# Packed attention before two gated layers: V in long runs, exponentials turned on VectorE, six weight tiles kept on chip

## The chip, the cores and the metric

The kernel runs on one core of one Trainium2 chip. The metric is device time in microseconds (us) of one execution. Five engines run their own in-order queues: TensorE (PE; its weight loads are shown apart as PEld), VectorE (DVE), ScalarE (ACT), GpSimd (POOL) and SyncE (SP), which here issues every copy. Copies run on 16 copy engines beside them.

## What is computed

In float32 inputs, q, k and v are [8, 8, 576, 64] (batch, heads, rows, columns), p is [8, 8, 32, 64]; the weights come in as 8-byte floats and are narrowed on the chip.

```python
def sm_attn(qq, kk, vv):
    s = scale * np.matmul(qq, kk.transpose(0, 1, 3, 2))
    s = s - np.max(s, axis=-1, keepdims=True)
    a = np.exp(s)
    a = a / (np.sum(a, axis=-1, keepdims=True) + 1e-09)
    return np.matmul(a, vv)
p_packed = sm_attn(p, k, v)            # 32 packed rows for each head
out = sm_attn(q, p_packed, p_packed)
x = out.transpose(0, 2, 1, 3).reshape(4608, 512)
xn = x / sqrt(mean(x * x) + 1e-6) * rms_g
x = (silu(xn @ w_gate) * (xn @ w_val)) @ w_out
h = x @ w2_in
result = (h * cos(h)) @ w2_out
```

## The kernel before

The work comes in three parts. The first part turns k, v and p into the packed rows: 16 groups, each of four heads of one batch. The second is the main loop, 192 steps (8 batches x 12 slices of 128 hidden columns x 2 halves of 288 tokens), whose matmuls are the gv products (L173 to L175 by the helper `mm3`) and the acc products. The third is the second layer (hx, ops).

The first part's order is written out by hand: `KEY_ORD` is a list of words, and each word calls one small step. For group i: `K` and `V` load k and v, `p` and `o` turn p and copy it to `pT`, `k` and `q` transpose k on TensorE in three pieces (L411) and evict each by ScalarE (L418), `s` makes the scores (L430, L434), `m` their maximum on VectorE (L441), `e` the exponential on ScalarE (L448), `t` and `T` transpose the exponentials on TensorE (L457) in two blocks of three and evict them by ScalarE (L463), `r` makes the reciprocal of the sum, `P` the product with v (L477), `C` scales it (L485), `f`, `F` and `G` turn it (L493) and put it away. Other words serve the main loop: `L` loads a piece of weights, `a` and `b` narrow it (one ScalarE pass, three VectorE passes, L160 to L168), `c` and `d` split a piece of w_out in two parts, `A` is one step of the second attention of batch 0, `U` makes one unit of batch 0's projected weights (mps, L606), `Z` issues the stores that wait, among them the narrowed weight tiles `wy` (L619), which later batches fetch again. The words are executed in the order of the list, so that every engine's queue and SP's queue hold their instructions in that order.

V is loaded into one of three tiles of 128 partitions, at partitions 16 to 111: 96 partitions with runs of six rows, 1536 bytes for each head (L376). The rest of a V tile and the margins of the one tile of exponentials are zeroed once, and each transpose of `t` takes 128 columns of which 96 are keys. The products of `P` run over 128 partitions, and four heads go to four column groups of the array. The first `S_PAD` = 6 groups make their scores with padded weights (128 columns, L430), the later ones with 32 columns for each head (L434). Float32 products are two instructions each.

Every `wy` tile lives in a ring of four buffers and is stored as soon as it is narrowed. In the main loop, `U_AT` says in which step a unit is made, `B0_W` which piece of weights is loaded and narrowed in which of the first steps, `ATT_FROM0` and `ATT_TO0` between which steps the next batch's attention is spread.

Of the kernel before, what the change touches and what calls it, by code (L numbers as in the profile page):

```python
# [20 lines left out]
def kernel(  # L21
# [39 lines left out]
    V_P = 16  # L61
# [3 lines left out]
    S_PAD = 6  # L65
    KEY_ORD = (
# [17 lines left out]
    )  # L84
    KEY_END = "b13 b14"
    U_AT = {3: (0, 3), 8: (0, 4), 14: (0, 5), 16: (1, 0), 18: (1, 1), 20: (1, 2), 22: (1, 3), 26: (1, 4), 30: (1, 5)}
    U_J = (12, 15, 18, 21, 26, 30)
    B0_W = (15, 16, 17, 18, 19, -4, 20, 21, -5, 22, 23, -6, 0, -7, 0, -8, 0, -9, 0, -10, 0, -11)
# [12 lines left out]
    ATT_FROM, ATT_TO, ATT_FROM0, ATT_TO0, N_ATT = 0, 48, 10, 45, 32  # L101
# [17 lines left out]
    c_dram = [dram.tile([128, 2, D], F32, name=f"c_{b}") for b in range(B)]  # L119
# [112 lines left out]
    def att_load_c(b):  # L232
        nc.sync.dma_start(out=cl, in_=c_dram[b])

    def attend(b):
        NB = HALF // NP
        s = a1.tile([128, 2, 2, NB, NP], F32, tag="s", name="s")
        for g in range(2):
            qTs = []
            for j in (2 * g, 2 * g + 1):  # L240
                qv = qn.pop(4 * b + j)
                qT = a2.tile([128, 2, HALF], F32, tag="qT", name="qT")
                for i in range(2):
                    tp = psb[0].tile([128, HALF], F32, tag="mm", name="qtp")
                    for c in range(CH):
                        nc.tensor.transpose(
                            tp[:, c * CP:(c + 1) * CP], qv[:, i, 2 * c:2 * c + 2, :].rearrange("p c d -> p (c d)"),
                            ident[:CP, :CP],
                        )
                    nc.scalar.activation(out=qT[:, i], in_=tp, func=AF.Copy)  # L250
                    qTs.append(qT[:, i])
                    if i == 0:
                        yield
                if b:
                    load_q()
                yield
            sp = [psb[0].tile([128, HALF], F32, tag="mm", name="sp") for _ in range(2)]
            for h in range(4):
                for r, rows in enumerate((top, bot)):
                    nc.tensor.matmul(  # L260
                        sp[r][h * NP:(h + 1) * NP], bq[rows, 4 * g + h], qTs[h ^ g][rows], start=True, stop=True
                    )
            st = a2.tile([128, 2, NB, NP], F32, tag="st", name="st", bufs=1)
            for r in range(2):
                nc.vector.transpose(st[:, r].rearrange("p c n -> p (c n)"), sp[r])
            yield
            sv = st.rearrange("p r c n -> p (r c) n")
            mx = a2.tile([128, 2 * NB], F32, tag="amx", name="amx")
            nc.vector.tensor_reduce(out=mx, in_=sv, op=ALU.max, axis=AX.X)
            nc.vector.tensor_tensor(  # L270
                out=s[:, g].rearrange("p r c n -> p (r c) n"), in0=sv,
                in1=mx.unsqueeze(2).to_broadcast([128, 2 * NB, NP]), op=ALU.subtract,
            )
            yield
# [77 lines left out]
    v_t = [u2.tile([128, 4, NC_, D], F32, tag=f"vn{x}", name="vn", bufs=1) for x in range(3)]  # L352
    for x in range(2):
        nc.vector.memset(v_t[x], 0.0)
    e_pad = u2.tile([128, 2 * V_P + S], F32, tag="e", name="e", bufs=1)
    for x in (slice(0, V_P), slice(V_P + S, 2 * V_P + S)):
        nc.vector.memset(e_pad[:, x], 0.0)
# [13 lines left out]
    def load_v(i):  # L371
# [3 lines left out]
        vn = nat_v[i] = v_t[i % len(v_t)]  # L375
        nc.sync.dma_start(out=vn[V_P:V_P + CP], in_=v[b, 4 * g:4 * g + 4].rearrange("h (p c) d -> p h c d", c=NC_))  # L376

# [3 lines left out]
    for x, y in ((slice(0, 4), slice(0, 4)), (slice(4, 8, 2), slice(5, 8, 2)), (slice(5, 8, 2), slice(4, 8, 2))):  # L381
        nc.gpsimd.tensor_copy(gS[:, x], gT[:, y])
# [14 lines left out]
    def u_pt(i):  # L397
        pt = st[i]["pt"]
        if i % 2:
            pv, tv = (x.rearrange("p (j r) n -> p j r n", r=2) for x in (pT[:, :, :NP], pt.rearrange("p (h n) -> p h n", h=4)))  # L400
            for r in range(2):
                nc.vector.tensor_copy(pv[:, :, r], tv[:, :, 1 - r])
        else:
            nc.vector.tensor_copy(pT[:, :, :NP], pt.rearrange("p (h n) -> p h n", h=4))
# [10 lines left out]
    def u_kt(i, m):  # L415
        z = st[i]
        kv = z["kT"].rearrange("q h (t p m) -> q h t m p", t=CH, m=CH)
        nc.scalar.activation(  # L418
            out=kv[:, :, :, m, :], in_=z["kp", m].rearrange("q (t h p) -> q h t p", t=CH, h=4), func=AF.Copy
        )  # L420

    def u_s1(i):
# [4 lines left out]
        for h in range(4):  # L427
            for r, rows in enumerate((top, bot)):
                if i < S_PAD:
                    nc.tensor.matmul(  # L430
                        s1[:, r, :HALF], pz[rows, h * 128:(h + 1) * 128], kT[rows, h ^ i % 2], start=h == 0, stop=h == 3
                    )
                else:
                    nc.tensor.matmul(  # L434
                        s1[h * NP:(h + 1) * NP, r, :HALF], pT[rows, h, :NP], kT[rows, h ^ i % 2], start=True, stop=True
# [8 lines left out]
    def u_e(i):  # L444
        z = st[i]
        s1, mx = z["s1"], z["mx"]
        e = e_pad[:, V_P:V_P + S].rearrange("p (a s) -> p a s", a=2)
# [4 lines left out]
    def u_et(i, hf):  # L452
        z = st[i]
        et = z["et", hf] = ps_2.tile([128, CH, 128], F32, tag="kp", name="et")
        for c in range(CH):
            cc = hf * CH + c
            nc.tensor.transpose(et[:, c, :], e_pad[:, cc * CP:cc * CP + 128], ident)  # L457

    def u_ec(i, hf):
        z = st[i]  # L460
        if hf == 0:
            z["eT"] = u2.tile([128, NC_, 128], F32, tag="eT", name="eT", bufs=1)
        nc.scalar.activation(out=z["eT"][:, hf * CH:(hf + 1) * CH], in_=z["et", hf], func=AF.Copy)  # L463
# [6 lines left out]
    def u_pp(i):  # L470
# [3 lines left out]
        for c in range(NC_):  # L474
            for h in range(4):
                r = slice(h * NP, (h + 1) * NP)
                nc.tensor.matmul(  # L477
                    pp[r], eT[:, c, r], vn[:, h ^ i % 2, c % CH * 2 + c // CH, :], start=c == 0, stop=c == NC_ - 1
                )

    def u_c(i):
# [6 lines left out]
        stores.append((c_dram[b][:, g, :], cd[:, 0, :]))  # L488
# [47 lines left out]
    def wy_prep(n, part, x=None):  # L536
        t, j = divmod(n, 2)
        if j == 0 and part == 0:
            w_y[t] = wm_p.tile([128, 2, 512], F32, tag="wy", name="wy", bufs=4)
# [3 lines left out]
        if j and part and x in (None, 3):  # L543
            stores.append((wy_dram[t], w_y[t]))
# [52 lines left out]
    def unit(b, u):  # L597
# [4 lines left out]
        for j in range(2):  # L602
            for r, rows in enumerate((top, bot)):
                for kt in range(2):
                    h = 2 * j + (1 - r if kt else r)
                    nc.tensor.matmul(  # L606
                        ps[kt][h * NP:(h + 1) * NP], ppT[b // 4][rows, 4 * kt + h, n:n + NP],
# [13 lines left out]
    stores = []  # L621
# [9 lines left out]
    def att0_load():  # L631
# [5 lines left out]
        "p": u_prep, "o": u_pt, "k": u_kp, "q": u_kt, "s": u_s1, "m": u_mx, "e": u_e, "t": u_et, "T": u_ec, "r": u_r,  # L637
# [11 lines left out]
    nc.gpsimd.memset(v_t[2], 0.0)  # L649
# [298 lines left out]
    for i in range(len(seq) + LAG):  # L948
# [27 lines left out]
        store(0)  # L976
        if i in units:
# [277 lines left out]
```

## Time and profile before

| | |
|---|---|
| median of three runs | 1615.98 us (1612.12 to 1622.82) |
| profiled execution | 1617.2 us |
| its span, first to last instruction | 1615.4 us |
| mean granted TensorE clock | 0.99 of full speed |
| first gv product of the main loop | 130.34 us after the span's start |

A profile page gives the busy time of each engine, then the costliest groups of instructions by line. A line of the trace names the line of the kernel, the engine, the operation, the tile written and the tiles read, partitions x elements, and a count. "Idle before" is the engine's idle time just before an instruction, with what ended it. A copy's share of 1.00 means that all 16 copy engines are busy all the time; shares can come out a little over 1 because packets overlap.

### The profile page before, as it was taken

Reading aid. Unit: us, or ns where it says so; the run is one execution under the profiler, and the core shown is the slowest. Engines: PE = TensorE matmul, PEld = TensorE weight load, DVE = VectorE, ACT = ScalarE, POOL = GpSimd, SP = SyncE. Lnnn points to the kernel's source line nnn. Section 1 sums busy time; section 2 is a strip of 40 time slices with the busy share of each in tenths; the row PEclk is TensorE's granted clock in tenths of the full one; section 3 lists DMA queues with packets and bytes.
Section 4 is the critical chain, followed back from the end, with each engine's and each line's share of the span. In section 5 each row is a group of like instructions: output and inputs, shape, how many; then the busy total and the mean of one; then the engine's idle time right before and its main releaser. Section 6 shows DMA issues by size and latency. Waiting matters only on the chain.

```text
span 1615.4 us, 28947 instructions
## 1 busy us (share of the span) xinstructions
PE 1570.9 (97%) x11216; PEld 1337.4 (83%) x11216; DVE 977.0 (60%) x1915; ACT 897.8 (56%) x1796; POOL 34.0 (2%) x49
## 2 busy tenths in 40 slices
PE   6878999999999999999999999999999999999998
PEld 4547778888888787888988999999999999999997
DVE  2788866666666766666525655555565555656544
ACT  4765545544545454454425666666666666666654
POOL 1000110000000000000000000000000000000000
PEclk9989999999999999999999999999999999999999
DMA  9998543655555565645457464646564645465451
GB/s 263 286 297 297 185 155 118 197 171 173 184 186 172 171 197 178 202 152 186 149 206 280 170 235 184 225 156 224 196 222 183 220 177 212 181 222 195 169 196 53
DMA packets 139321, 315.96 MB, mean 196 GB/s; under 512 B 42800, under 2 KB 61232, under 8 KB 132912
## 3 DMA queue, kind: packets, MB, share of 16 engines
q1 hardware_dynamic: 139184, 314.11, 58.2%
q8 instruction: 89, 1.46, 0.4%
q14 instruction: 48, 0.39, 0.1%
HBM read 262.15 MB, written 51.90 MB: 194 GB/s over the span
## 4 chain that ended last, share of the span: by engine, by line
PE 85%; DMA 1%; issue 1%; DVE 1%; ACT 0%; POOL 0%; SPq 0%; POOLq 0%; DVEq 0%; ACTq 0%
PE ops L173 8%; PE ops L174 8%; PE ops L175 8%; PE gv L173 6%; PE acc L173 6%; PE gv L174 5%; PE gv L175 5%; PE acc L175 5%; PE acc L174 5%; PE hx L175 4%; PE hx L174 4%; PE hx L173 4%; PE mps L606 2%; PE hz L175 2%; PE hz L174 2%; PE hz L173 2%
## 5 line engine op out<-in xcount | busy, mean ns | idle before, releaser
L173 PE MATMUL gv<-apt,wmhl 128*128 128x288 f32 x768 | 234.2, 305 | 1.6 <-ACT apt L129 0.9
L174 PE MATMUL gv<-apt,wmhl 128*128 128x288 f32 x768 | 228.1, 297 | 0.4 <-DVE apt L130 0.4
L175 PE MATMUL gv<-apt,wmhl 128*128 128x288 f32 x768 | 226.9, 295 | 0.0
L173 PE MATMUL ops<-w2hl,ghl 128*128 128x512 f32 x576 | 226.0, 392 | 0.0
L174 PE MATMUL ops<-w2hl,ghl 128*128 128x512 f32 x576 | 225.8, 392 | 0.0
L175 PE MATMUL ops<-w2hl,ghl 128*128 128x512 f32 x576 | 224.2, 389 | 0.1
L784 ACT ACTIVATE shl<-silu 128x288 fp32r<-128x288 f32 x192 | 85.4, 445 | 196.8 <-DVE silu L777 194.0
L173 PEld LDWEIGHTS gv<-apt,wmhl 128*128 128x128 f32 x768 | 145.2, 189 | 48.3 <-issue 17.3
L173 PE MATMUL acc<-shl,wohl 128*128 128x512 f32 x432 | 175.7, 407 | 1.0 <-ACT wohl L569 0.9
L175 PE MATMUL acc<-shl,wohl 128*128 128x512 f32 x432 | 170.4, 395 | 2.7 <-POOL wohl L572 2.7
L174 PE MATMUL acc<-shl,wohl 128*128 128x512 f32 x432 | 169.8, 393 | 0.0
L175 PE MATMUL hx<-xhl,wab 128*128 128x256 f32 x576 | 163.0, 283 | 0.0
L174 PE MATMUL hx<-xhl,wab 128*128 128x256 f32 x576 | 162.9, 283 | 0.0
L173 PE MATMUL hx<-xhl,wab 128*128 128x256 f32 x576 | 162.3, 282 | 0.5 <-ACT u L1183 0.5
L174 PEld LDWEIGHTS gv<-apt,wmhl 128*128 128x128 f32 x768 | 145.3, 189 | 6.0 <-DVE apt L130 0.6
L777 DVE TENSOR_TENSOR silu<-silu,gv 128x288 f32<-128x288 f32 x192 | 86.4, 450 | 99.6 <-PE gv L175 68.1
L175 PEld LDWEIGHTS gv<-apt,wmhl 128*128 128x128 f32 x768 | 145.1, 189 | 0.0
L175 PEld LDWEIGHTS ops<-w2hl,ghl 128*128 128x128 f32 x576 | 108.2, 188 | 24.1 <-DVE ghl L1073 0.5
L173 PEld LDWEIGHTS ops<-w2hl,ghl 128*128 128x128 f32 x576 | 108.7, 189 | 19.0 <-ACT ghl L1069 0.2
L174 PEld LDWEIGHTS ops<-w2hl,ghl 128*128 128x128 f32 x576 | 108.7, 189 | 17.2
L1069 ACT ACTIVATE ghl<-r 128x512 fp32r<-128x512 f32 x144 | 90.5, 628 | 54.6 <-DVE r L1065 54.6
L173 PEld LDWEIGHTS hx<-xhl,wab 128*128 128x128 f32 x576 | 110.0, 191 | 6.6 <-ACT u L1183 1.0
(148 smaller groups left out, 3220.8 us busy)
## 6 DMA issues: line engine op xcount, KB each, us to landing
wab<-wa SPq DMA_DIRECT2D x49, 1024.0 KB, 4.8
wy<-wy SPq DMA_DIRECT2D x96, 512.0 KB, 4.6
wab<-wb SPq DMA_DIRECT2D x49, 768.0 KB, 6.5
wab<-wa SPq DMA_DIRECT2D x46, 512.0 KB, 5.3
wab<-wb SPq DMA_DIRECT2D x69, 256.0 KB, 4.9
kn<-in_k_dram SPq DMA_DIRECT2D x16, 576.0 KB, 8.9
vn<-in_v_dram SPq DMA_DIRECT2D x16, 576.0 KB, 9.2
qnat<-in_q_dram SPq DMA_DIRECT2D x32, 288.0 KB, 3.9
```

The costliest lines, as they stand in the source:

```text
L173: nc.tensor.matmul(ps, lhi, rhi, start=first, stop=False, skip_group_check=chain)
L174: nc.tensor.matmul(ps, lhi, rlo, start=False, stop=False, skip_group_check=chain)
L175: nc.tensor.matmul(ps, llo, rhi, start=False, stop=last, skip_group_check=chain)
L606: nc.tensor.matmul(ps[kt][h * NP:(h + 1) * NP], ppT[b // 4][rows, 4 * kt + h, n:n + NP], w_y[2 * u + kt][rows, j], start=True, stop=True,)
L777: nc.vector.tensor_tensor(out=t, in0=t, in1=pss[1], op=ALU.mult)
L784: nc.scalar.activation(out=sh[:, 0, cols], in_=t, func=AF.Copy)
L1069: nc.scalar.activation(out=g[:, 0], in_=h_t[q]["r", s], func=AF.Copy)
```

## The change

V is loaded like K: 128 partitions, (head, 32 row groups), each with one run of 18 rows, 4608 bytes, in one of four tiles. The exponentials have two tiles without margins. `t` is gone; `T` is now one VectorE instruction that transposes the 128x576 exponentials in blocks of 32x32. `P` multiplies over 32 keys: 18 chunks, each with four products of 32 partitions by 32 columns, one for each head, on the array's diagonal. k's columns are laid in the same order. The head swap of odd groups goes from p, k and v to the places where the packed rows are read again (`c` is stored with a new layout and loaded by five copies instead of one; the swapped head index in `attend` and `unit`). Only the first two groups have padded scores.

The first six `wy` tiles are taken from the `wm` ring (12 buffers) and stored not in the first part but in steps 0, 6 and 8 of the main loop, two tiles each. `KEY_ORD` holds the same words but for the 32 `t`, and 16 `T` in place of 32, in a new order; `U_AT`, `B0_W` and `ATT_FROM0` are shifted by some steps.

```diff
-    S_PAD = 6
+    VB, EB = 4, 2
+    S_PAD = 2
     KEY_ORD = (
...
-        "F0 G0 k3.2 P1 C1 q3.2 a0 Z K6 b0 s3 t2.0 T2.0 t2.1 r2 m3 T2.1 p4 k4.0 k4.1 Z a1 Q q4.1 V4 f1 q4.0 F1 G1 o4 "
+        "V2 P0 Q e1 Q q2.2 V3 s2 L2 C0 T1 p3 k3.0 m2 o3 V4 f0 e2 k3.1 q3.1 q3.0 r1 Z k3.2 P1 F0 C1 G0 r2 q3.2 s3 T2 a0 "
...
-    U_AT = {3: (0, 3), 8: (0, 4), 14: (0, 5), 16: (1, 0), 18: (1, 1), 20: (1, 2), 22: (1, 3), 26: (1, 4), 30: (1, 5)}
+    U_AT = {4: (0, 3), 13: (0, 4), 14: (0, 5), 15: (1, 0), 19: (1, 1), 21: (1, 2), 24: (1, 3), 27: (1, 4), 29: (1, 5)}
+    U_K, H_AT = 3, (0, 6, 8)
-    B0_W = (15, 16, 17, 18, 19, -4, 20, 21, -5, 22, 23, -6, 0, -7, 0, -8, 0, -9, 0, -10, 0, -11)
+    B0_W = (15, 16, 17, 18, 19, -4, -5, 20, 21, 22, -6, 23, 0, -7, -8, -9, 0, 0, -10, 0, -11, 0)
-    ATT_FROM, ATT_TO, ATT_FROM0, ATT_TO0, N_ATT = 0, 48, 10, 45, 32
+    ATT_FROM, ATT_TO, ATT_FROM0, ATT_TO0, N_ATT = 0, 48, 6, 46, 32
...
     def att_load_c(b):
-        nc.sync.dma_start(out=cl, in_=c_dram[b])
+        nc.sync.dma_start(out=cl[:, 0], in_=c_dram[b][0, 0])
+        for h in range(4):
+            nc.sync.dma_start(out=cl[h * NP:(h + 1) * NP, 1], in_=c_dram[b][1, 0, (h ^ 1) * NP:((h ^ 1) + 1) * NP])
...
-        vn = nat_v[i] = v_t[i % len(v_t)]
-        nc.sync.dma_start(out=vn[V_P:V_P + CP], in_=v[b, 4 * g:4 * g + 4].rearrange("h (p c) d -> p h c d", c=NC_))
+        vn = nat_v[i] = u5.tile([128, CH * NC_, D], F32, tag="vn", name="vn", bufs=VB)
+        nc.sync.dma_start(out=vn, in_=v[b, 4 * g:4 * g + 4].rearrange("h (p c) d -> (h p) c d", c=CH * NC_))
...
     def u_pt(i):
-        pt = st[i]["pt"]
-        if i % 2:
-            pv, tv = (x.rearrange("p (j r) n -> p j r n", r=2) for x in (pT[:, :, :NP], pt.rearrange("p (h n) -> p h n", h=4)))
-            for r in range(2):
-                nc.vector.tensor_copy(pv[:, :, r], tv[:, :, 1 - r])
-        else:
-            nc.vector.tensor_copy(pT[:, :, :NP], pt.rearrange("p (h n) -> p h n", h=4))
+        nc.vector.tensor_copy(pT[:, :, :NP], st[i]["pt"].rearrange("p (h n) -> p h n", h=4))
...
-    def u_et(i, hf):
-        z = st[i]
-        et = z["et", hf] = ps_2.tile([128, CH, 128], F32, tag="kp", name="et")
-        for c in range(CH):
-            cc = hf * CH + c
-            nc.tensor.transpose(et[:, c, :], e_pad[:, cc * CP:cc * CP + 128], ident)
-
-    def u_ec(i, hf):
-        z = st[i]
-        if hf == 0:
-            z["eT"] = u2.tile([128, NC_, 128], F32, tag="eT", name="eT", bufs=1)
-        nc.scalar.activation(out=z["eT"][:, hf * CH:(hf + 1) * CH], in_=z["et", hf], func=AF.Copy)
+    def u_et(i):
+        z = st[i]
+        z["eT"] = u2.tile([128, 2, HALF // NP, NP], F32, tag="eT", name="eT", bufs=1)
+        nc.vector.transpose(z["eT"].rearrange("p a c n -> p (a c n)"), z["e"].rearrange("p a s -> p (a s)"))
...
-        for c in range(NC_):
+        n_c = CH * NC_
+        for c in range(n_c):
             for h in range(4):
                 r = slice(h * NP, (h + 1) * NP)
-                nc.tensor.matmul(
-                    pp[r], eT[:, c, r], vn[:, h ^ i % 2, c % CH * 2 + c // CH, :], start=c == 0, stop=c == NC_ - 1
-                )
+                nc.tensor.matmul(pp[r], eT[r, c % 2, c // 2], vn[r, c], start=c == 0, stop=c == n_c - 1)
...
         if j == 0 and part == 0:
-            w_y[t] = wm_p.tile([128, 2, 512], F32, tag="wy", name="wy", bufs=4)
+            if t < 2 * U_K:
+                w_y[t] = wm_p.tile([128, 2, 512], F32, tag="wm", name="wy")
+            else:
+                w_y[t] = wm_p.tile([128, 2, 512], F32, tag="wy", name="wy", bufs=4)
...
-            stores.append((wy_dram[t], w_y[t]))
+            (held if t < 2 * U_K else stores).append((wy_dram[t], w_y[t]))
...
         store(0)
+        if i in H_AT:
+            stores.extend(held[:2])
+            del held[:2]
+            store(0)
         if i in units:
```

## Rows read from the trace of the kernel before

**Rows 1.** The page's first part: busy time, share of the span, instructions.

```profile
PE 1570.9 (97%) x11216; PEld 1337.4 (83%) x11216; DVE 977.0 (60%) x1915; ACT 897.8 (56%) x1796; POOL 34.0 (2%) x49
```

**Rows 2.** Busy time by stretch; 12.75 and 44.79 start the first and fifth maximum (L441).

```profile
core 0: us, PE busy (x) PEld busy (x) DVE busy (x) ACT busy (x) POOL busy (x), PEclk, DMA share, GB/s
0.00:12.75 12.75, 6.73 (x27) 4.64 (x28) 2.92 (x6) 3.24 (x4) 4.02 (x20) 1.00 0.86 220
12.75:44.79 32.04, 25.65 (x280) 18.49 (x281) 8.90 (x33) 14.73 (x32) 0.95 (x4) 0.84 1.07 278
44.79:79.16 34.37, 28.76 (x534) 19.14 (x531) 27.37 (x72) 28.17 (x66) 2.15 (x5) 1.00 1.05 292
79.16:103.94 24.78, 18.58 (x275) 10.90 (x275) 21.66 (x54) 16.86 (x37) 1.06 (x3) 0.79 1.06 303
103.94:130.34 26.40, 18.05 (x333) 11.77 (x334) 20.61 (x54) 17.14 (x41) 1.79 (x2) 0.94 0.96 282
130.34:200.00 69.66, 67.11 (x469) 53.45 (x470) 60.78 (x116) 39.62 (x84) 5.59 (x4) 0.95 0.74 243
200.00:300.00 100.00, 98.49 (x718) 78.37 (x718) 65.18 (x131) 49.25 (x107) 8.94 (x6) 1.00 0.47 152
```

**Rows 3.** TensorE's waits up to 130.34 us: total, times, longest.

```profile
PE kp L411 <- ACT eT L463: 4.3, 3, 2.4
...
PE kp L411 <- DMA kn<-in_k_dram: 2.4, 1, 2.4
```

**Rows 4.** Timeline about 94 us, TensorE and ScalarE: start, length, instruction, idle before.

```profile
94.44 0.90 PE L457 MATMUL et<-ident,e 128*128 128x128 f32 x3 [2.15 <-ACT e L448]
...
93.56 0.74 ACT L448 ACTIVATE e<-s,mx 128x576 f32<-128x576 f32 x1 [0.91 <-DVE mx L442]
```

**Rows 5.** Copy packets of 46 to 48, 90 to 92 and 122 to 126 us.

```profile
DMA packets 325, 0.44 MB, mean 221 GB/s; under 512 B 70, under 2 KB 313, under 8 KB 325
...
DMA packets 358, 0.78 MB, mean 388 GB/s; under 512 B 184, under 2 KB 198, under 8 KB 358
...
DMA packets 780, 1.61 MB, mean 403 GB/s; under 512 B 312, under 2 KB 413, under 8 KB 780
```

**Rows 6.** Copy issues up to 130 us: count, size of one, us to landing.

```profile
vn<-in_v_dram SPq DMA_DIRECT2D x16, 576.0 KB, 9.2
...
wy<-wy SPq DMA_DIRECT2D x6, 512.0 KB, 8.3
```

**Rows 7.** Timeline of TensorE, single blocks: start, length, instruction.

```profile
48.12 2.21 PE L430 MATMUL s<-kT,pT 64*128 64x288 f32 x16
...
60.44 0.72 PE L434 MATMUL s<-kT,pT 64*32 64x288 f32 x16
...
67.91 0.88 PE L457 MATMUL et<-ident,e 128*128 128x128 f32 x6
...
70.91 0.88 PE L477 MATMUL pp<-vn,eT 128*32 128x64 f32 x48
...
106.26 0.71 PE L305 MATMUL xp<-at,cl 32*64 32x288 f32 x8
...
405.39 1.09 PE L606 MATMUL mps<-wy,ppT 64*32 64x512 f32 x16
```

**Rows 8.** Groups by line up to 130.34 us: busy us, mean ns, idle before.

```profile
L457 PE MATMUL et<-ident,e 128*128 128x128 f32 x96 | 16.6, 307 | 5.5 <-ACT e L448 4.5 <-ACT kT L418 1.1
L477 PE MATMUL pp<-vn,eT 128*32 128x64 f32 x768 | 15.6, 233 | 1.5 <-ACT eT L463 1.3
L463 ACT ACTIVATE eT<-et 128x384 f32<-128x384 f32 x32 | 14.5, 489 | 21.7 <-PE et L457 21.6
...
L402 DVE COPY pT<-pt 128x64 f32<-128x64 f32 x16 | 2.8, 214 | 4.3 <-PE pt L394 4.3
...
L404 DVE COPY pT<-pt 128x128 f32<-128x128 f32 x8 | 2.2, 275 | 0.0
...
L294 DVE STREAM_TRANSPOSE at<-s 128x576 f32<-128x576 f32 x2 | 1.5, 770 | 0.0
```

More of the change, by code (lines that the diff above doesn't have):

```diff
@@ L60 @@
     REST = S - 512
-    V_P = 16
+    VB, EB = 4, 2
     S_AT = (20, 21, 24 + 1, 24 + 2)
@@ L117 @@
     magic = const.tile([128, 1], F32, name="magic")
-    c_dram = [dram.tile([128, 2, D], F32, name=f"c_{b}") for b in range(B)]
+    c_dram = [dram.tile([2, 2, 128, D], F32, name=f"c_{b}") for b in range(B)]
     q_dram = [dram.tile([128, H, NP], F32, name=f"q_{b}") for b in range(B)]
@@ L260, in attend @@
                     nc.tensor.matmul(
-                        sp[r][h * NP:(h + 1) * NP], bq[rows, 4 * g + h], qTs[h ^ g][rows], start=True, stop=True
+                        sp[r][h * NP:(h + 1) * NP], bq[rows, 4 * g + (h ^ g)], qTs[h ^ g][rows], start=True, stop=True
                     )
@@ L350, in attend @@
             yield nxt[:1]
[L352 to L357, printed above, removed]
     nat_k, nat_v = {}, {}
@@ L380 @@
         nc.sync.dma_start(out=gT[i * 64:(i + 1) * 64, :], in_=rms_g.rearrange("(h d) -> d h", d=D))
-    for x, y in ((slice(0, 4), slice(0, 4)), (slice(4, 8, 2), slice(5, 8, 2)), (slice(5, 8, 2), slice(4, 8, 2))):
-        nc.gpsimd.tensor_copy(gS[:, x], gT[:, y])
+    nc.gpsimd.tensor_copy(gS, gT)
     load_k(1)
@@ L416, in u_kt @@
         z = st[i]
-        kv = z["kT"].rearrange("q h (t p m) -> q h t m p", t=CH, m=CH)
+        kv = z["kT"].rearrange("q h (c p) -> q h c p", p=NP)
         nc.scalar.activation(
-            out=kv[:, :, :, m, :], in_=z["kp", m].rearrange("q (t h p) -> q h t p", t=CH, h=4), func=AF.Copy
+            out=kv[:, :, CH * m:CH * (m + 1), :], in_=z["kp", m].rearrange("q (t h p) -> q h t p", t=CH, h=4), func=AF.Copy
         )
@@ L430, in u_s1 @@
                     nc.tensor.matmul(
-                        s1[:, r, :HALF], pz[rows, h * 128:(h + 1) * 128], kT[rows, h ^ i % 2], start=h == 0, stop=h == 3
+                        s1[:, r, :HALF], pz[rows, h * 128:(h + 1) * 128], kT[rows, h], start=h == 0, stop=h == 3
                     )
@@ L434, in u_s1 @@
                     nc.tensor.matmul(
-                        s1[h * NP:(h + 1) * NP, r, :HALF], pT[rows, h, :NP], kT[rows, h ^ i % 2], start=True, stop=True
+                        s1[h * NP:(h + 1) * NP, r, :HALF], pT[rows, h, :NP], kT[rows, h], start=True, stop=True
                     )
@@ L446, in u_e @@
         s1, mx = z["s1"], z["mx"]
-        e = e_pad[:, V_P:V_P + S].rearrange("p (a s) -> p a s", a=2)
+        e = z["e"] = u2.tile([128, 2, HALF], F32, tag="e", name="e", bufs=EB)
         nc.scalar.activation(
@@ L487, in u_c @@
         )
-        stores.append((c_dram[b][:, g, :], cd[:, 0, :]))
+        stores.append((c_dram[b][g, 0], cd[:, 0, :]))
     def u_tp(i):
@@ L606, in unit @@
                     nc.tensor.matmul(
-                        ps[kt][h * NP:(h + 1) * NP], ppT[b // 4][rows, 4 * kt + h, n:n + NP],
+                        ps[kt][h * NP:(h + 1) * NP], ppT[b // 4][rows, 4 * kt + 2 * j + r, n:n + NP],
                         w_y[2 * u + kt][rows, j], start=True, stop=True,
@@ L619, in store @@
             nc.sync.dma_start(out=dst, in_=src)
-    stores = []
+    stores, held = [], []
     wm_t = {}
@@ L636 @@
         "K": load_k, "V": load_v, "Q": load_q, "L": w_load, "B": b0_load, "X": att0_load, "Z": lambda: store(0),
-        "p": u_prep, "o": u_pt, "k": u_kp, "q": u_kt, "s": u_s1, "m": u_mx, "e": u_e, "t": u_et, "T": u_ec, "r": u_r,
+        "p": u_prep, "o": u_pt, "k": u_kp, "q": u_kt, "s": u_s1, "m": u_mx, "e": u_e, "T": u_et, "r": u_r,
         "P": u_pp, "C": u_c, "f": u_tp, "F": u_tf, "G": u_g, "A": att0, "U": lambda u: unit(0, u),
@@ L648 @@
         u_kt(0, m)
-    nc.gpsimd.memset(v_t[2], 0.0)
     def do(words):
```

30 rows, old and new, of the table KEY_ORD are left out of this document.

## The prediction, on record before the changed kernel ran

> **What bounds the kernel now.** I read the page's busy shares first: TensorE is busy 1570.9 of 1615.4 us [rows 1], so whatever does not shorten TensorE's work or its idle time brings nothing. The table by stretch says where that idle time is [rows 2]. Until the first gv product at 130.34 us TensorE is busy 6.73 + 25.65 + 28.76 + 18.58 + 18.05 = 97.8 us, so idle 32.5; in the next 70 us it is idle 2.55 us. Nearly everything that can be won lies in the first 130 us, the part that the change rewrites.
>
> What holds that part? TensorE's own waits name ScalarE's evictions and hardly a copy [rows 3]; but the copy queue's share is 1.05 to 1.07 in every stretch from 12.75 to 103.94, that is, all 16 copy engines never rest [rows 2]. The list was laid out so that data come just in time, and what the copies take sets its pace. VectorE is next: 27.37 + 21.66 + 20.61 = 69.64 us in the 85.55 us from 44.79 on (81%), 87% in 79.16 to 103.94. One wait shows it: a list step's exponential starts at 93.56 after 0.91 us of waiting on VectorE's maximum, and the transposes behind it at 94.44 after 2.15 us of TensorE idleness [rows 4].
>
> **Copies.** Three stretches differ in what moves. From 46 to 48 us, with 313 - 70 = 243 of 325 packets between 512 and 2048 bytes (V and q are the loads with 1536-byte runs), the queue moved 221 GB/s; at 90 to 92, almost without them (14), 388; at 122 to 126, 403 [rows 5]. V is 16 copies of 576 KB, 9.44 MB [rows 6]: at 221 GB/s 42.7 us of queue time, at 388 it would be 24.3, a gain of 18.4. K has the shape that V gets (4608-byte runs over 128 partitions). Six 512 KB stores (3.15 MB) leave the first part [rows 6]: 8 us at 388 GB/s. The queue's 130 us thus fall to about 104 us if the run length is what counts, and to 122 us if it is not; I take 104, as the rows without 1536-byte runs are so far off. The stores come back in steps 0, 6 and 8 of the main loop, where 8 us fit beside a share of 0.74 over 69.66 us [rows 2].
>
> The Trainium skill (DMA: Bandwidth & Descriptors, Specifications) gives 512 B as the least transfer for line rate; by it 1536-byte runs would gain nothing from being longer, and the sum would be 122 us. The 221 against 388 GB/s speaks against it here.
>
> **TensorE.** Out go 96 transposes: a block of six takes 0.88 us, one 0.31 [rows 7, 8], so a further one costs (0.88 - 0.31)/5 = 0.11 and a block 0.68; 16 blocks, -11 us. The products with V go from 12 to 36 rounds of four (six key chunks of 96 become 18 of 32, two passes each). A block of 48 instructions took 0.88 us at 0.23 each, so a round costs (0.88 - 0.23)/11 = 0.059, and 36 rounds 35 x 0.059 + 0.23 = 2.3 us: +1.42 x 16 = +22.7. This needs the four 32x32 tiles of a round to run together. Two rows bound it: four 32-row tiles do in xp (8 instructions of 288 columns in 0.71 us), and eight 64x32 tiles do in mps (16 of 512 columns in 1.09 us) [rows 7], where upper and lower rows write different partitions of one PSUM bank, as the new tiles will. Were they to run singly, 144 x 0.059 + 0.2 = 8.7 us a block. I take 2.3. Four of the padded score products become tiled: 2.21 against 0.72 us [rows 7], -6. TensorE's sum in the part is -11 + 22.7 - 6 = +6, beside 32.5 us of idleness: no bound, but it takes part of the slack.
>
> The Trainium skill (TensorEngine Tiling (Array Packing), Restrictions and Gotchas) says that different row tiles write different PSUM banks and cannot access one bank at the same time; by it the 8.7 us would hold. The mps row stands against it for different partitions of one bank.
>
> **ScalarE** loses 32 evictions of 0.489 us [rows 8], 14.5 us; its kT evictions, for which TensorE waited, come sooner.
>
> **VectorE** gains 16 block transposes. The same operation on 128x576 stands in the trace at 0.770 us [rows 8]: +12.3. Eight odd groups save a second head copy, 2 x 0.214 against 0.275: -1.2. (The zero fills of V's and the exponentials' padding go too; VectorE idles there anyway.) From 44.79 on, with 12 of the groups to come, that is 12 x 0.770 - 6 x 0.15 = +8.3, so 77.9 us in place of 69.64. What is queued behind a transpose is the next maximum or a weight's three passes, and behind the maximum the exponential, then TensorE's next products. The transpose is listed one group after its exponential, and the exponentials get two buffers, so it waits for nothing itself.
>
> **The sum.** Two stretches. From the first maximum to the fifth (12.75 to 44.79, 32.0 us) VectorE has 8.9 us of work, so it is no bound; TensorE has 25.65, less three padded savings (4.5), less four et blocks (2.7), plus some three longer products (4.3), so 22.7, and the copies' 278 x 32.0 = 8.9 MB take 23 us at 388 GB/s. It cannot go under 23 us and should not exceed 31; I take 24, -8. From there to the first gv product VectorE's 77.9 us decide. At the mean density of before (81%) they take 95.8 us, +10.3; at its densest (87%, and the same in 130 to 200 us [rows 2]) 89.2, +3.7; at 95% 82, -3.5. I take 90%, 86.6 us, +1: a little over the densest, since ScalarE and the copies, which fed it late, both get lighter. In the main loop the weights' narrowing is reordered, with w_out's pieces a step or two earlier: of TensorE's 2.55 us idle there I count 1 back. The four further issues for the c load cost SP a few tenths each (8 times); SP issues ahead and TensorE is idle only 1.5 us in 200 to 300 us, so nothing. Together -8 + 1 - 1 = -8 us. The profiled execution took 1617.2 us, 1.2 over the median; so 1617.2 - 8 - 1.2 = 1608 us.
>
> **Rivals.** (1) The copies were all: VectorE packs at 95% and the start shrinks to 23 us: -9 - 3.5 - 2.5 in the main loop = -15, and up to -18 if weights move to the idle start; 1599 us. For it: a queue that never rests; against it: no stretch shows VectorE at 95%. (2) The gain is eaten: VectorE stays at 83%, 93.9 us, +8.3 against -8 at the start; 1616 us. For it: VectorE is an in-order queue and got 12 us more; against it: its named waits were on ScalarE, which is relieved. (3) The runs bring nothing, by the copy rule above: the queue needs 122 us in the part, just under what VectorE leaves; then the start shrinks by 2 to 4 us at most and the end is 1614 us. The 221 GB/s rows speak against it. (4) The other side: the four tiles of a round share a bank and take turns. At 8.7 us a block TensorE gets 16 x 7.8 = 125 - 17 = 108 us more against 32.5 idle: some +75, 1690 us. Two at a time (72 rounds, 4.4 us) give +56 - 17 = +39 against 32.5, about 1625. It decides once a block costs more than some 4 us, 17 + 32.5 = 49.5 over 16 blocks being 3.1 above today's 0.88.
>
> **How the numbers follow.** Forecast 0.50 (own range 1602 to 1614), (1) 0.19, (2) 0.19, (3) 0.05, (4) 0.07. The range 1596 to 1621 takes in all but the end of (1) and most of (4), together under 2 in 10. About 1% (16 us) is what a measurement of this kernel can tell from no change. Under 1599.8 lie nearly all of (1) and little else: 0.20. Over 1632 lies most of (4): 0.06. The rest, 0.74, is within 1%.
>
> **What would show it.** In the profile after: V copies in the queue's fast stretches and the copy share in 13 to 104 us well under 1 (else rival 3); a product block of 48 x 3 instructions in about 2.3 us (4.4 or 8.7: rival 4); block transposes of 0.77 us on VectorE and VectorE over 88% busy from the fifth group's maximum on, with TensorE's and ScalarE's waits now naming it (else rival 1); the first gv product near 123 us (130: rival 2; 115: rival 1); TensorE without new idle time after it. I am wrong if the start does not shrink although its copies come early, which would mean that the chain from keys to exponentials, not copies or TensorE, set its pace.

## The result, and the profile after

The changed kernel takes 1641.82 us (median of six runs, 1639.16 to 1642.87), the kernel before in the same comparison 1620.45 us (six runs, 1612.12 to 1622.82). The ratio is 1.0141, with a 95% interval of 1.012 to 1.0162: slower by 1.4%, where 1608 us was forecast with an upper end of 1621.

The profiled execution took 1641.4 us with a span of 1639.6, 24.2 longer than the 1615.4 of before. From the page of after, the busy line that answers to [rows 1], and the line of copy queue q8, which brings TensorE's own instructions (packets, MB, share):

```profile
PE 1578.1 (96%) x12656; PEld 1350.5 (82%) x12656; DVE 982.2 (60%) x1919; ACT 877.6 (54%) x1764; POOL 31.4 (2%) x46
...
q8 instruction: 100, 1.64, 0.4%
```

The same q8 line on the page of before:

```profile
q8 instruction: 89, 1.46, 0.4%
```

The table by stretch of after answers to [rows 2]. The first maximum starts at 12.63, the fifth at 43.43, the first gv product at 158.23 us (columns as there):

```profile
0.00:12.63 12.63, 6.91 (x27) 4.62 (x28) 0.29 (x1) 2.76 (x4) 2.54 (x17) 1.00 0.82 264
12.63:43.43 30.80, 20.02 (x565) 15.26 (x569) 11.27 (x34) 10.76 (x27) 0.95 (x4) 0.94 0.85 278
43.43:158.23 114.80, 81.26 (x2310) 58.66 (x2298) 77.51 (x185) 46.88 (x114) 3.70 (x10) 0.82 0.59 199
158.23:200.00 41.77, 41.38 (x287) 36.06 (x288) 37.16 (x74) 26.38 (x53) 2.58 (x2) 0.96 0.93 316
200.00:300.00 100.00, 98.98 (x735) 77.67 (x734) 71.22 (x141) 51.15 (x112) 10.08 (x7) 1.00 0.50 168
```

All of the loss lies ahead of the first gv product, which comes 27.9 us later (158.23 against 130.34). From there to the end after is 3.7 us shorter (1481.4 against 1485.1). Up to the first gv product TensorE is busy for 6.91 + 20.02 + 81.26 = 108.2 us and idle for 50.0; before it was 97.8 and 32.5 [rows 2]. So 10.4 us are more busy time and 17.5 are more idle time. Nothing else is full: the copies' share fell to 0.85 and 0.59, VectorE is at 77.51 of 114.80 us (68%).

What does TensorE wait for? Its waits up to 158.23 us (total, times, longest) name a releaser that [rows 3] does not have:

```profile
PE pp L458 <- issue: 20.3, 8, 5.4
PE s L422 <- issue: 6.4, 2, 3.6
PE pt L388 <- POOL pn L386: 3.8, 2, 2.8
```

"issue" means that the engine waited for nothing that the profile shows: no data, no other engine. The timeline of TensorE shows where these waits fall (start, length, instruction, idle before):

```profile
26.13 0.92 PE L422 MATMUL s<-kT,pT 64*32 64x288 f32 x3 [3.64 <-issue]
...
34.23 0.65 PE L458 MATMUL pp<-vn,eT 32*32 32x64 f32 x31 [2.74 <-issue]
...
37.98 2.21 PE L458 MATMUL pp<-vn,eT 32*32 32x64 f32 x144
...
87.31 1.77 PE L458 MATMUL pp<-vn,eT 32*32 32x64 f32 x112
92.95 1.08 PE L458 MATMUL pp<-vn,eT 32*32 32x64 f32 x32 [3.88 <-issue]
...
123.28 2.21 PE L458 MATMUL pp<-vn,eT 32*32 32x64 f32 x142
130.84 0.42 PE L458 MATMUL pp<-vn,eT 32*32 32x64 f32 x2 [5.35 <-issue]
```

A product block that runs through at the full clock takes 2.21 us. Others stop in the middle, after 112 or 142 of 144 products of the same data, which cannot be a wait for an operand. Setting the packets of q8 beside TensorE's instructions (weight loads, products and the queue's semaphore instructions, counted from the start) explains the places. Each q8 packet has 16,384 bytes, and nine of the ten waits stand right behind instruction numbers 449, 705, 1473, 1729 and so on, always 193 plus a multiple of 256: one packet is 256 instructions of 64 bytes, here called a piece. The count fits the whole run: 100 packets are 25,600 instructions, and TensorE's queue executed 25,654. At each of these nine stops, 25.2 of the 26.7 us, TensorE goes on 1.3 to 1.6 us after a packet has landed. And at all 22 boundaries the transfer of a packet, which takes about 1 us, starts only after TensorE has entered the piece before it, 0.4 to 6.7 us later. TensorE waits for its own code.

The tenth wait is of another kind. It stands inside a piece, at the head of a block, and ends 0.11 us after VectorE has turned that block's exponentials, although the profile names no releaser:

```profile
42.31 0.77 DVE L443 STREAM_TRANSPOSE eT<-e 128x576 f32<-128x576 f32 x1
...
43.19 2.56 PE L458 MATMUL pp<-vn,eT 32*32 32x64 f32 x144 [1.43 <-issue]
```

### The profile page after: what moved, and what is told of

It reads as the page before. It is cut to its first block, busy times and chain, and to the rows that moved or that the text cites. A ratio compares the mean times of both kernels' runs of the same rounds, so it can differ in the third digit from the quotient of the medians.

```text
span 1639.6 us, 31834 instructions
## 1 busy us (share of the span) xinstructions
PE 1578.1 (96%) x12656; PEld 1350.5 (82%) x12656; DVE 982.2 (60%) x1919; ACT 877.6 (54%) x1764; POOL 31.4 (2%) x46
## 4 chain that ended last, share of the span: by engine, by line
PE 87%; DMA 1%; ACT 1%; DVE 1%; issue 0%; SPq 0%; DVEq 0%; ACTq 0%
PE ops L172 8%; PE ops L173 8%; PE ops L174 8%; PE gv L172 7%; PE gv L173 6%; PE gv L174 6%; PE acc L172 6%; PE acc L173 6%; PE acc L174 6%; PE hx L174 4%; PE hx L173 4%; PE hx L172 4%; PE mps L588 3%; PE hz L174 2%; PE hz L173 2%; PE hz L172 2%
## 5 line engine op out<-in xcount | busy, mean ns | idle before, releaser
L174 PEld LDWEIGHTS ops<-w2hl,ghl 128*128 128x128 f32 x576 | 108.2, 188 | 24.1 <-DVE ghl L1058 0.5
```

What stands on the lines that cost most here:

```text
L174: nc.tensor.matmul(ps, llo, rhi, start=False, stop=last, skip_group_check=chain)
```

## The experiments

Each theory is named in the expectations: A, code loading; B, the small array tiles or the clock; C, VectorE's queue. The counts of this section up to each kernel's first gv product, worked out from the packets of q8 and TensorE's instructions as above:

| kernel | first gv, us | code pieces | median us of TensorE per piece | median us from entering a piece to the next one's transfer | pieces on which TensorE went on within 1.8 us of the landing |
|---|---|---|---|---|---|
| before | 130.34 | 10 | 10.1 | 3.2 | 0 |
| after | 158.23 | 22 | 6.1 | 2.6 (up to 6.7) | 14 |
| e1_wide | 128.09 | 10 | 10.0 | 2.4 | 0 |
| e2_third | 122.44 | 10 | 10.5 | 3.1 | 0 |
| e3_thrice | 170.51 | 22 | 6.3 | 2.0 (up to 6.2) | 11 |
| e4_split | 160.7 | 21 | 6.0 | 1.7 (up to 6.7) | 8 |
| e5_few_loads | 143.90 | 21 | 5.1 | 1.3 (up to 7.2) | 10 |

**e1_wide: the same column time in a third of the instructions.** The kernel after, with six rounds of 192 columns instead of 18 of 64:

```diff
-        n_c = CH * NC_
+        n_c = NC_
...
-                nc.tensor.matmul(pp[r], eT[r, c % 2, c // 2], vn[r, c], start=c == 0, stop=c == n_c - 1)
+                nc.tensor.matmul(pw[r], eT[r, c % 2, c // 2], vn[r, 3 * c:3 * c + 3], start=c == 0, stop=c == n_c - 1)
```

> The changed kernel, but each group's product with v is made of 6 rounds of 192 columns instead of 18 of 64: about the same TensorE column time (12 passes of about 0.18 us), a third of the instructions (96 instead of 288 a group). It leaves the right sum of v out (columns 64 to 191 are extra, two thirds of the keys are missing). Theory A, the instructions of the product outrun the loading of TensorE's code: the gaps put down to issue in TensorE's stream (26 us after the change) fall under 6 us, the first gv product comes at 126 to 134 us instead of 158, total 1609 to 1618. Theory B, products of 32 keys cost TensorE's time or its clock: first gv product stays at 152 to 160, total 1634 to 1643. Theory C, VectorE's queue with the transposes sets the pace: as B, 1634 to 1643.

Measured: 1613.94 us, ratio to before 0.9972 (0.9956 to 0.9987). Its table by stretch, from the first maximum and from the fifth:

```profile
12.66:35.84 23.18, 17.71 (x268) 12.32 (x272) 11.14 (x33) 10.62 (x27) 0.89 (x4) 1.00 1.05 344
35.84:128.09 92.25, 69.47 (x1063) 41.52 (x1055) 76.70 (x185) 46.69 (x114) 4.29 (x11) 0.93 0.74 253
```

One product block of its timeline:

```profile
30.46 2.15 PE L459 MATMUL pp<-vn,eT 32*32 32x192 f32 x48
```

The block takes the same time (2.15 against 2.21 us), on the same 32x32 tiles, with VectorE doing the same; only the instructions went from 288 to 96 a block. The waits by issue fall from 27 to 4.1 us and 28 us of the time go with them. None of the three that are left stands at the end of a piece: the blocks start at 35.61, 42.94 and 49.54 us, each 0.10 us after a transpose by VectorE has ended. So no wait for code is left. The first gv product at 128.09 us, and not at 152 to 160, rules out C, and B for the small tiles. The clock keeps a share: up to the first gv product e1 is idle for 34.0 us and busy for 94.1, where after is idle for 50.0 and busy for 108.2, and the mean granted clock is 0.95 against 0.86.

**e2_third: a third of the products.** The kernel after with six of the 18 key chunks (`n_c = NC_`, nothing else).

> The changed kernel with only 6 of the 18 key chunks of each product with v (two thirds of the keys are left out): a third of the instructions and a third of the column time. Theory A: as with the wide products, less what 16 x 1.4 = 22 us of TensorE's time in blocks still cost when they are not hidden, 1602 to 1616. Theory B: 1605 to 1616 here alone, and not with the wide products. Theory C: 1634 to 1643.

Measured: 1606.78 us, 0.9936 (0.99 to 0.9973). TensorE's column time in the products falls as well, and the first gv product comes at 122.44 us. From its fifth maximum on:

```profile
33.61:122.44 88.83, 63.58 (x1062) 39.38 (x1050) 76.72 (x185) 46.91 (x115) 4.92 (x11) 0.75 0.79 272
```

The granted clock of 0.75 here is lower than after's 0.82 over the same part, and yet the part ends 36 us sooner: a low clock by itself does not make it long. (A third of the products' columns helps here too, so this separates clock from code less sharply than e1 does.)

**e3_thrice: the kernel before with the instruction count of after.** Each product of before is made three times over, each time from a fresh start, so that the output stays the same; transposes, V copies and list are those of before.

```diff
-        for c in range(NC_):
+        for c in [c for _ in range(3) for c in range(NC_)]:
```

> The kernel before, with each product with v made three times over (each time from a fresh start, so the output is the same): 288 instructions a group as after the change, over 128 partitions as before, everything else untouched. Theory A: gaps put down to issue appear in TensorE's stream, 15 to 30 us of them, and the total goes from about 1618 to 1632 to 1650. If only TensorE's time counts (16 x 1.4 = 22 us against 32 us of idleness): 1618 to 1628, with issue gaps under 5 us. Theory C: no change beyond that.

Measured: 1655.71 us, 1.0242 (1.0199 to 1.0285). TensorE's waits up to its first gv product at 170.51 us:

```profile
PE pp L477 <- issue: 19.5, 7, 6.3
PE s L430 <- issue: 3.8, 1, 3.8
...
PE et L457 <- issue: 3.4, 1, 3.4
```

26.7 us of waits by issue, all nine of them at the ends of pieces, arise in a kernel that has none of the change's parts, in products over 128 partitions. It even passed A's upper end. The products' column time rises here as well, from 15.6 us [rows 8] to 38.4, for which the expectation alone allowed up to 1628 us. With e1, which holds the columns and cuts the count, this settles the cause from both sides.

**e4_split: the blocks cut in three.** The kernel after with each product block (but the first two and the last two) in three parts of 96 instructions, the first two behind the key transposes of a later group, so that TensorE has longer instructions between them.

```diff
+        if part == 0:
+            z["pp"] = ps_2.tile([128, D], F32, tag="kp", name="pp")
...
+        for c in range(NC_ * part, NC_ * (part + 1)):
```

> The changed kernel with each product with v cut into three parts of 96 instructions, the first two put earlier in the list behind the key transposes of the group two further on; the sum of the work is the same. Theory A: the loading of code gets more time between the parts, issue gaps fall to 8 to 16 us, total 1622 to 1632. Theory B and C: 1636 to 1646, since TensorE's and VectorE's work is the same.

Measured: 1646.74 us, 1.0187 (1.014 to 1.0233), which A had not expected. Waits up to its first gv product:

```profile
PE pp L462 <- issue: 14.5, 6, 4.1
PE s L424 <- issue: 5.6, 2, 3.2
PE pp L462 <- DVE eT L445: 4.9, 5, 1.7
```

The waits by issue shrink only from 27 to 20 us. But 12.2 us of these stand at the ends of pieces, where after had 25.2, and that is inside A's 8 to 16. The other 7.9, at 44.20, 61.99 and 98.37 us, each end 0.10 us after a transpose by VectorE, as the longest shows:

```profile
97.50 0.77 DVE L445 STREAM_TRANSPOSE eT<-e 128x576 f32<-128x576 f32 x1
...
98.37 1.50 PE L462 MATMUL pp<-vn,eT 32*32 32x64 f32 x48 [4.13 <-issue]
```

So A was right about the code and wrong about the total: products listed earlier meet exponentials that VectorE has not turned yet. Where the rest of the gain went was not followed up.

**e5_few_loads: why a piece is late.** The kernel after with k and v loaded for four groups only.

```diff
+        if i >= VB:
+            nat_v[i] = vn_0[i % VB]
+            return
```

> The kernel after with k and v loaded for the first four groups only; the twelve later groups compute on those tiles again, so their packed rows are not those of the inputs. 24 copies of 576 KB (14.2 MB, some 36 us of queue time at 390 GB/s) leave the first part; TensorE's instructions stay what they are (288 a product block). Theory A1 (pieces of TensorE code come late because they queue among the copies): with the copy engines free a piece starts within about 1 us, TensorE's waits put down to issue fall from 34 to under 12 us in the first part, the first gv product comes at 128 to 138 us and the time is 1612 to 1624 us. Theory A2 (a piece takes its 4 to 8 us by itself, whatever else is copied): the issue waits stay between 22 and 34 us, the first gv product at 148 to 158 us and the time at 1632 to 1642 us.

Measured: 1628.86 us, 1.0067 (1.0043 to 1.0091), between the two bands. TensorE's waits up to 143.90 us:

```profile
PE pp L465 <- issue: 9.2, 5, 4.4
...
PE s L429 <- issue: 4.1, 1, 4.1
...
PE rp L322 <- issue: 2.3, 1, 2.3
```

Its stretch from 36 us on:

```profile
36.00:143.90 107.90, 79.00 (x2478) 57.83 (x2477) 80.43 (x193) 48.87 (x119) 4.11 (x11) 0.87 0.36 110
```

15.6 us of waits by issue remain at a copy share of 0.36, 14.2 of them at the ends of pieces, against 25.2 in after. (The 34 us of the expectation are not the 26.7 of TensorE's products shown above.) So both hold: among many copies a piece starts late (median 2.6 against 1.3 us), and even without them a piece needs about 1.3 us to start, 1 to land and 1.3 until TensorE goes on, 3.6 us, while the products use 256 instructions in 2.0 us (2.21 x 256 / 288).

**e6_held and e7_held_pad2: the copies' part alone.** The kernel before with the six tiles on chip (e6), and with `S_PAD = 2` besides (e7).

```diff
-            stores.append((wy_dram[t], w_y[t]))
+            (held if t < 2 * U_K else stores).append((wy_dram[t], w_y[t]))
...
-    S_PAD = 6
+    S_PAD = 2
```

> The kernel before with one part of the change alone: six narrowed tiles stay on chip and are stored in steps 0, 6 and 8 of the main loop, with the unit, weight and attention steps shifted as in the change; list, V copies, transposes and products as before. Theory 1 (copies set the pace of the first part): 3.1 MB less, 8 us of queue time at 388 GB/s, first gv product at 122 to 126 us, 1608 to 1613 us. Theory 2 (the chain through VectorE, ScalarE and TensorE sets it, the list being the same): first gv product at 128 to 131 us, 1614 to 1620 us. If the shifted steps of the main loop cost something by themselves, it shows as TensorE idle time after 200 us, beyond the 27 us of before.

> As e6_held, and only the first two groups make their scores with padded weights (four blocks of 2.21 us become 0.72 us, 6.0 us of TensorE in the start stretch). Theory 1 (copies and TensorE set the pace of the start, as the prediction's sum of that stretch had it): up to 6 us below e6_held, 1603 to 1611 us, fifth maximum 4 to 8 us earlier than e6_held's. Theory 2 (the chain from keys to exponentials sets it): within 2 us of e6_held.

Measured: e6 1613.81 us, 0.9961 (0.9949 to 0.9973); e7 1613.31 us, 0.9967 (0.9954 to 0.9981). Of the versions with the whole computation these two are the only ones faster than both kernels, by some 0.4%. The first gv product of e6 comes at 128.70 us, not at 122 to 126: theory 1 overstated what 8 us of queue time are worth. Of the 5.7 us by which e6's profiled span is shorter than before's, only 1.6 lie ahead of that product. e7 adds nothing. TensorE's busy time in the whole run falls by 6.8 us, and one wait takes its place, in the waits of e7 to 200 us:

```profile
PE kp L412 <- ACT eT L464: 7.6, 3, 6.2
```

This wait names ScalarE, but a copy stands behind it. The eviction was queued behind a ScalarE pass that narrows weights, and that pass waited for the weights' copy, 7.09 us in e7:

```profile
34.19 0.66 ACT L153 ACTIVATE wy<-wo 128x512 f32<-128x512 f32 x1 [7.09 <-DMA wo<-in_moe_w_gate_dram]
```

In before the same pass waited 4.79 us:

```profile
34.54 0.66 ACT L152 ACTIVATE wy<-wo 128x512 f32<-128x512 f32 x1 [4.79 <-DMA wo<-in_moe_w_gate_dram]
```

So in this place the copies set the pace, as the prediction had it, and what TensorE saved was waited for.

**e8_v_from_0: the place of V's partitions.** The kernel before with `V_P = 0`.

> The kernel before with the 96 partitions of V at 0 to 95 instead of 16 to 111, runs of 1536 bytes as before. If the slow V copies (221 GB/s) come from the length of the runs, stretches with V copies stay at 200 to 240 GB/s and the time at 1614 to 1622 us. If they come from the place of the 96 partitions among the copy engines' 128, the stretches change to another rate (over 280 or under 180 GB/s).

Measured: 1618.51 us, 0.9992 (0.9974 to 1.001). V's copies of the part up to 130 us (count, size, us to landing) land as slowly as in [rows 6], where after's take 6.4 us:

```profile
vn<-in_v_dram SPq DMA_DIRECT2D x16, 576.0 KB, 9.4
```

Between the first and the fifth maximum the queue moved 274 GB/s, against 278 in [rows 2]. The place plays no part.

**e9_key_order and e10_key_order_held: ScalarE's share.** k's columns without gaps, on before (e9) and on e6 (e10); V then comes in three copies of 32 partitions for each group.

```diff
-        kv = z["kT"].rearrange("q h (t p m) -> q h t m p", t=CH, m=CH)
+        kv = z["kT"].rearrange("q h (t m p) -> q h t m p", t=CH, m=CH)
...
+        for m in range(CH):
+            nc.sync.dma_start(
+                out=vn[V_P + m * NP:V_P + (m + 1) * NP],
+                in_=v[b, 4 * g:4 * g + 4].rearrange("h (p m c) d -> m p h c d", m=CH, c=NC_)[m],
+            )
```

> The kernel before with k's columns in the order in which ScalarE can write them without gaps (32 in a row, as the change has 96), and V therefore loaded in three copies of 32 partitions for a group, runs of 1536 bytes as before. The profile of after has the key eviction at 492 ns where before had 698, 48 of them in the first part: 9.9 us of ScalarE. Theory 1 (the chain through ScalarE's evictions sets the pace of the first part before, as TensorE's named waits say): first gv product 4 to 10 us earlier than 130, 1606 to 1614 us. Theory 2 (the copies set it, 1.05 of the queue): nothing, or up to 4 us slower if 32 partitions at a time copy worse: 1615 to 1622 us.

> Both edits that leave TensorE's instructions as they are: six narrowed tiles on chip (as e6_held, measured at 0.9961 of before) and the key order of e9_key_order. Theory 1 (ScalarE's evictions): e9's gain on top of e6's 6 us, 1602 to 1609 us. Theory 2 (copies): about e6's time, 1611 to 1617 us. If both bound by turns, the gain is more than the sum of the two alone.

Measured: e9 1628.45 us, 1.0049 (1.0032 to 1.0065); e10 1618.59 us, 0.9995 (0.998 to 1.0011). The eviction's group in before, up to 130.34 us:

```profile
L418 ACT ACTIVATE kT<-kp 128x384 f32<-128x384 f32 x48 | 31.8, 698 | 11.1 <-PE kp L411 11.0
```

The same group in e9, up to 130 us:

```profile
L422 ACT ACTIVATE kT<-kp 128x384 f32<-128x384 f32 x48 | 22.8, 495 | 13.7 <-PE kp L415 12.9
```

It falls by 9 us in all, but ScalarE then waits 13.53 us for the weight copy that kept it for 4.79 in before, as its timeline shows:

```profile
40.32 0.66 ACT L152 ACTIVATE wy<-wo 128x512 f32<-128x512 f32 x1 [13.53 <-DMA wo<-in_moe_w_gate_dram]
```

The queue moved 250 GB/s up to 130 us against 282 before, so the three narrow copies cost more than the 9 us of ScalarE gave: the first gv product comes at 142.06 us in e9 and at 131.33 in e10. Both kernels went past their expected ranges upward. What the eviction alone would bring was not tried.

## Why the prediction was wrong

**The step that failed** is the one on TensorE: the products' cost was worked out as 36 x 0.059 us of column time, and the sum of +6 us was set beside 32.5 us of idleness with the words "no bound". The column time was right for a block at the full clock: 2.21 us against 2.3. Five of the blocks that ran through took longer, up to 4.06 us at a granted clock of 0.50 (1.2 of 2.4 GHz), and all sixteen came to 43.4 us where 16 x 2.3 are 36.8, in the groups of after up to 158.23 us:

```profile
L458 PE MATMUL pp<-vn,eT 32*32 32x64 f32 x2304 | 43.4, 234 | 25.1 <-issue 20.3 <-DVE eT L443 2.3 <-ACT wy L151 0.9
...
L406 ACT ACTIVATE kT<-kp 128x384 f32<-128x384 f32 x48 | 22.6, 492 | 52.1 <-PE kp L399 51.5
L443 DVE STREAM_TRANSPOSE eT<-e 128x576 f32<-128x576 f32 x16 | 12.2, 764 | 0.0
...
L464 DVE TENSOR_SCALAR cd<-pp,mx 128x128 f32<-128x128 f32 x16 | 5.5, 346 | 31.8 <-PE pp L458 31.8
```

What was not costed, and so stood in the sum at nothing, is the supply of instructions. The counts were at hand: x768 for the products in [rows 8], three times as many after, each with a weight load. That is 16 x 192 = 3072 more instructions less 192 for the transposes, on some 2,900 up to the first gv product. At 256 to a piece that is 11 more pieces, and the nine waits at the ends of pieces, none over 5.4 us, add up to 25.2 us of idle time. In before the tightest piece landed 2.0 us ahead of its need, and e8, with before's instructions, has one wait at the end of a piece (1.9 us at 74.73), so three times the rate had no room.

The Trainium skill (Runtime: NRT & Kernel Launch, Instruction fetch mechanics) says that instructions are refilled in 16 KiB blocks of 256 while the current block executes, and that crossing a block is mostly hidden. The packets here agree with the block's size; that the crossing is hidden holds for before and e1, and not for after, where the nine waits come to 25.2 us in 22 crossings.

**Copies: right.** Share times length, summed up to the first gv product, is 133 us of a full queue in before [rows 2], 104 in after and 103 in e1; 104 were forecast. In e1, where the code waits are gone, the start stretch moves 344 GB/s at a share of 1.05, against 278 at 1.07 before [rows 2], and the later share is 0.74; the sign that was named for it, a share well under 1, holds for the later part alone. V's longer runs on more partitions count; which of the two, e8 and e9 do not tell, as e9's narrower copies at the same run length were slower too. So rival 3 falls.

**The start stretch: right without the code waits.** e1 needs 23.2 us between the first and the fifth maximum; 24 were forecast. That is in part luck: 344 GB/s for 23.2 us are 8.0 MB, where 8.9 MB at 388 had been reckoned, TensorE was busy for 17.7 us and not 22.7, and e2 needs 20.95 us, less than the 23 that were held to be the least. In after two stops of 3.64 and 2.74 us and what they delay make it 30.8.

**VectorE: work right, density wrong.** Its work from the fifth maximum on is 77.51 us in after and 76.70 in e1; 77.9 were forecast. The block transposes take 764 ns (forecast 770). But e1 needs 92.25 us for it, 83% and not 90%, and that is rival 2's density; the 95% of rival 1 is seen nowhere over that part, e2's 86% being the highest. Without the code waits the change would thus have come out near e1's 1614 us as far as e1 can stand for it: 6 above the forecast, inside the range, and nearer to rival 2's 1616. In after VectorE is no bound, it waits 31.8 us for the products (the last line above).

**Rival 4** (the four tiles of a round take turns) falls with the 2.21 us. Its sign was right and its place too, TensorE's products, by another mechanism; its point of decision, more than some 4 us a block, was reached through waits: (43.4 + 25.1) / 16 = 4.3 us.

**The main loop** was to give 1 us back, and it is 3.7 us shorter. But from its first gv product to the end the kernels with the shifted steps take 1480.1 to 1485.4 us, and those without 1483.4 to 1485.2, so not even the sign is shown.

**ScalarE** got more than forecast: not only 32 evictions went, but k's column order made the 48 that stay 0.2 us shorter each, 492 against 698 ns. With TensorE stopped that brought nothing: these evictions wait 51.5 us for the key transposes.

**Open:** why a piece's transfer starts up to 7.2 us late even in e5, and whether the stops brought the granted clock down. The 10.4 us of additional busy time go with that clock in the main: the 144 key transposes, the same in both, take 27.8 us in after and 23.7 in e1, where the clock from the fifth maximum on is 0.93 against 0.82. But e2, which has no waits at the ends of pieces, has 0.75 there. Products in one pass, which would halve their instructions, were not tried.

## What to carry to other kernels

Count a change's instructions, weight loads included, as well as its columns: where TensorE's instructions are short (0.008 us each here), divide the count by 256 and ask whether each such piece lasts longer than the 3.6 us, or under busy copies up to 9, that the next one needs. A wait put down to "issue" in the middle of a block of like products is the sign; at the head of a block such a wait can be another engine's, as VectorE's transposes showed here. The cause is confirmed by holding the columns and changing the count alone. Work that is split finer to suit a faster data path can lose on the way in of its own code.

## What the runs showed of the hardware

- TensorE's code comes in packets of 16,384 bytes, 256 instructions. A packet is on its way only after TensorE has entered the piece before it (0.4 to 6.7 us later in after), takes about 1 us, and TensorE goes on 1.2 to 1.6 us after it has landed.
- Those packets share the copy engines with data: with 24 copies of 576 KB left out the waits at the ends of pieces fell from 25.2 to 14.2 us.
- Four 32x32 tiles that write different partitions of one PSUM bank run together: 144 products in 2.21 us, where one after another they would take 8.7 by the prediction's estimate.
- ScalarE writes 128x384 from PSUM in 492 ns where runs of 32 or 96 elements are without gaps, and in 698 ns with every third element.
